# An RWKV-5 and sentence-level MoE kernel: opening re-ordered, logits read in PSUM, w1 loaded in two halves

## Chip, cores and metric

The kernel runs on one core of one Trainium2 chip. The metric is the device time of that core in microseconds (us), the median over several executions. Two parts of an execution are told apart throughout. The **opening** goes from the start to the first expert matmul job (called the first job below). The **packed part** goes from there to the end of the span. All moments are counted from the start of the span of the profiled execution; the span is some 1.7 us shorter than the device time. **Whole clock** and **half clock** are stretches in which the profile shows a granted TensorE clock of 1.0 and of 0.5. The **index** is the number of the chosen expert (`idx`), which the loads of w1 and w2 wait for.

## The reference

Four sequences of 768 steps with 8 heads of 48 run through a linear attention with decay; then each whole sequence goes to one of 8 experts. Cut to what matters:

```python
for t in range(S):                                   # S = 768
    cur = einsum('bhd,bhe->bhde', u[None] * k[t], v[t])
    y[:, :, t] = einsum('bhd,bhde->bhe', r[t], state + cur)
    state = w[None, :, :, None] * state + einsum('bhd,bhe->bhde', k[t], v[t])
x = y as (B, S, 384)
logits = x.mean(axis=1) @ w_gate                     # one expert for a whole sequence
e = argmax(logits); gate_w = softmax(logits)[e]
out = gate_w * (relu(x @ w1[e]) @ w2[e])             # w1 384x1024, w2 1024x384
```

## The kernel before

A sequence is cut into three groups of 256 steps, so there are twelve groups, 0 to 11, and four gates. For one group TensorE transposes the scaled k and r (`twp`), ScalarE copies the result to SBUF (`kr`), VectorE forms `prod` for the bonus, TensorE makes scores (`at`), VectorE masks them (`gt`), TensorE adds up y and the state `s`, VectorE forms the state `st`, ScalarE copies y (`xn`), and TensorE turns it back (`xp`, copied to `xt`). After the third group of a sequence the gate picks an expert. Its work is then cut into jobs of matmuls (`hp` for w1, `op` for w2), which fill TensorE while the next sequence's groups run.

The first sequence has no expert work to run beside it. There the author writes the order by hand and puts `fill` matmuls (zeros times zeros) into the gaps, meant to keep TensorE's clock up (in e5 below, with 19 more of them, half clock shrank from 20.5 us in e2 to 3.4).

```python
pp_tw  = tile_pool(bufs=1, space=PSUM)      # one bank: transposes, also xp
pp_at  = tile_pool(bufs=1, space=PSUM)
pp_moe = tile_pool(bufs=2, space=PSUM)      # two banks: hp, op, logits, fills, some twp
...
load(0); load(1)                            # each loads k, r, v of a group
wg = ...                                    # gate weights
for g in range(2, AHEAD): load(g)
fill(4, 512); ...; fill(7, 512)
...
def transposes(g, c):
    if c and g < NB + 2:                    # NB = 3: groups 0..4, second half, in pp_moe
        fill_bank()
        twp = pp_moe.tile(...)
    else:
        twp = pp_tw.tile(...)
    ...                                     # eight 128x128 transposes
    nc.scalar.copy(kts[g][:, :, :, c, :], tw)
    nc.vector.tensor_mul(prods[g][:, :, c], tw[:, 0:NP], rts[g][:, :, :, c, :])
...
def gate(b):
    lgp = pp_moe.tile([128, 512], FP32, tag="moe", name=f"lgp{b}")
    ...                                     # three small matmuls
    lg = gpool.tile([128, E], FP32, tag="lg", name=f"lg{b}")
    nc.vector.tensor_copy(lg, lgp[:, 0:E])
    nc.vector.max(out=top8, in_=lg)
    nc.vector.max_index(out=idx8, in_max=top8, in_values=lg)
def gate_weight(b):                         # in the packed part: after scores and bonus
    nc.vector.tensor_scalar_mul(negmax, top8[:, 0:1], -1.0 / S)
    nc.scalar.activation(out=exps, in_=lg, func=ACT.Exp, bias=negmax, scale=1.0 / S)
    ...
def mm1(b, w1, ht, ft, sb):                 # w1 is one tile [128, 3, 1024]
    nc.tensor.matmul(out=hp[:, 0:SB], lhsT=w1[:, ct, ft::NFT], rhs=...)   # NFT = 8
...                                         # the opening, cut to groups 0 to 3
prep(0); transposes(0, 0); transposes(0, 1); fill(4, 512); prep(1); scores(0, 0)
prep_v(0); ...; fill(5, 512); scores(0, 1); bonus(0, False); ...
transposes(1, 0); transposes(1, 1); scores_v(0, 1, True); ...
fill(3, 512); scores(1, 0); scores_v(0, 0, True); transposes(2, 0); fill(1, 512)
scores(1, 1); bonus(1); ...; transposes(2, 1); prep_v(2); fill(2, 512)
add_bonus(0); evac_y(0, 0); inter(0, 1); evac_y(0, 1)
scores(2, 0); scores_v(1, 1, True); backs(0); ...
prep_r(3); prep_v(3); ...                   # v of group 3 converted ahead of the gate
outputs(2, ...); pool_sum(0); transposes(3, 0); gate(0); weights(0); ...; gate_weight(0)
transposes(3, 1); fill(2, 256); scores(3, 0); fill(2, 256); scores(3, 1); bonus(3)
```

Of the kernel before, what the change touches and what calls it, by code (L numbers as in the profile page):

```python
# [18 lines left out]
def kernel(  # L19
# [52 lines left out]
    def load(g):  # L72
        b, gi = divmod(g, NB)
        for name, src in (("k32", k), ("r32", r), ("v32", v)):
            t = inp.tile([128, H, 2, D], FP32, tag=name, name=f"{name}_{g}")
            nc.sync.dma_start(
                out=t.rearrange("q h c d -> q h (c d)"),
                in_=src[b, :, L * gi : L * gi + L, :].rearrange("h (q c) d -> q h (c d)", c=2),
            )
            raw[name, g] = t  # L80
# [17 lines left out]
    load(0)  # L98
    load(1)
    wg = const.tile([128, NCT, E], FP32, tag="wg", name="wg")  # L100
    nc.sync.dma_start(out=wg, in_=moe_w_gate.rearrange("(p ct) e -> p ct e", p=128))
    for g in range(2, AHEAD):
        load(g)
# [16 lines left out]
    fill(7, 512)  # L120
# [75 lines left out]
    s_ps, xts, carry, tcols = {}, {}, {}, {}  # L196
# [31 lines left out]
    def transposes(g, c):  # L228
        if c and g < NB + 2:
            fill_bank()  # L230
            twp = pp_moe.tile([128, 2 * NP, 128], BF16, tag="moe", name=f"twp{g}_{c}")
        else:
            twp = pp_tw.tile([128, 2 * NP, 128], BF16, tag="tw", name=f"twp{g}_{c}")
        for o, src in ((0, kp[g % NR]), (NP, rp[g % NR])):
            for p in range(NP):
                nc.tensor.transpose(  # L236
                    out=twp[:, o + p, :],
                    in_=src[:, c, 2 * p : 2 * p + 2, :].rearrange("s a b -> s (a b)"),
                    identity=ident,
                )  # L240
        if c == 0:
            kts[g] = work.tile([128, 2 * NP, 2, 2, 64], BF16, tag="kr", name=f"kr{g}")
            rts[g] = kts[g][:, NP : 2 * NP]
            prods[g] = work.tile([128, NP, 2, 2, 64], BF16, tag="prod", name=f"prod{g}")
        tw = twp.rearrange("q o (j i) -> q o j i", j=2)
        nc.scalar.copy(kts[g][:, :, :, c, :], tw)  # L246
        nc.vector.tensor_mul(prods[g][:, :, c], tw[:, 0:NP], rts[g][:, :, :, c, :])  # L247
# [60 lines left out]

    def inter(g, j):
        st, rt = sts.pop((g, j)), rts[g]  # L310
        yj = ys[g][j]
        for p in range(NP):
            nc.tensor.matmul(  # L313
                out=yj[:, 96 * p : 96 * p + 96],
                lhsT=rt[:, p, j].rearrange("q c i -> q (c i)"), rhs=st[:, p, :],
                start=(j == 0 and p == 0), stop=False, skip_group_check=True,
            )
# [10 lines left out]
    def scores_v(g, j, first):  # L328

        gi = g % NB  # L330
        if j:
            ys[g] = [
                pp_y.tile([128, 512], FP32, tag=f"y{i}", name=f"y{i}_{g}") for i in range(2)]
        gt, vb, yj = gts[g], vbs[g], ys[g][j]
        o = 1 - j
        with_state = not (o == 1 and gi == NB - 1)
        if o == 0:
            b = g // NB
# [8 lines left out]
        sp = s_ps[g // NB]  # L347
        q, qo = slice(64 * j, 64 * j + 64), slice(64 * o, 64 * o + 64)

        def y_mm(i):  # L350
            h, c = divmod(i, 2)
            p, a = divmod(h, 2)
            nc.tensor.matmul(  # L353
                out=yj[:, D * h : D * h + D],
                lhsT=gt[q, p // 2, a, p % 2, c, :], rhs=vb[q, c, h, :],
                start=(first and i == 0), stop=(c == 1), skip_group_check=True,
            )

        def s_mm(i):
            p, c = divmod(i, 2)  # L360
# [4 lines left out]
                start=(gi == 0 and o == 0 and i == 0), stop=(c == 1), skip_group_check=True,  # L365
            )

        for i in range(H):
            y_mm(2 * i)
            if with_state:  # L370
                s_mm(i)
            y_mm(2 * i + 1)
        if not with_state:
            return
        st = work.tile([128, NP, 2 * D], BF16, tag="st", name=f"st{g}_{o}")
        nc.vector.tensor_mul(  # L376
            st, sp[:, 0 : 2 * D * NP].rearrange("q (p e) -> q p e", p=NP),
            wcmask if o else bmask.rearrange("q p a d -> q p (a d)"),
        )
        if o:  # L380
            carry[g // NB] = st
# [4 lines left out]
    def evac_y(g, j):  # L386
        if j == 0:
            xns[g] = work.tile([128, 2, DM], BF16, tag="xn", name=f"xn{g}")
        nc.scalar.copy(xns[g][:, j, :], ys[g][j][:, 0:DM])  # L389

    def backs(g):
# [3 lines left out]
        xn, sp = xns.pop(g), s_ps[b]  # L395
# [7 lines left out]
        for j in range(2):  # L403
            for ct in range(NCT):
                o = DM + 2 * NB * ct + 2 * gi + j
                nc.tensor.matmul(
                    out=sp[:, o : o + 1], lhsT=xn[:, j, ct::NCT], rhs=ones_col,
                    start=False, stop=True, skip_group_check=True,
                )
        nc.scalar.copy(xts[b][:, :, L * gi : L * gi + L], xp)  # L410
        for d in (vbs, kts, rts, prods, gts, vts, ys):
            d.pop(g, None)

# [13 lines left out]
    def gate(b):  # L427
# [7 lines left out]
        lg = gpool.tile([128, E], FP32, tag="lg", name=f"lg{b}")  # L435
        nc.vector.tensor_copy(lg, lgp[:, 0:E])  # L436
# [19 lines left out]
    jobs = []  # L456

    def weights(b):
        idx8 = gates[b][0]
        ev = nc.gpsimd.value_load(idx8[0:1, 0:1], min_val=0, max_val=E - 1)  # L460
        w1 = wpool.tile([128, NCT, F], BF16, tag="w1", name=f"w1_{b}")
        nc.gpsimd.dma_start(  # L462
            out=w1.rearrange("p ct f -> p (ct f)"),
            in_=moe_w1[ds(ev, 1)].rearrange("o (p ct) f -> p (o ct f)", ct=NCT))
        w2 = wpool.tile([128, NFT, DM], BF16, tag="w2", name=f"w2_{b}")
        nc.gpsimd.dma_start(
            out=w2.rearrange("p ft m -> p (ft m)"),
            in_=moe_w2[ds(ev, 1)].rearrange("o (p ft) m -> p (o ft m)", ft=NFT))
# [11 lines left out]
    def mm1(b, w1, ht, ft, sb):  # L480
        hp = pp_moe.tile([128, 512], FP32, tag="moe", name=f"hp{b}_{ft}_{sb}")
        for ct in range(NCT):
            nc.tensor.matmul(  # L483
                out=hp[:, 0:SB], lhsT=w1[:, ct, ft::NFT],
# [56 lines left out]
    def outputs(g, gaps=None):  # L541

        gaps = gaps or [lambda: None] * 3
        if g % NB:
            inter(g, 0)
        scores_v(g, 0, g % NB == 0)
        add_bonus(g)
        evac_y(g, 0)
        gaps[0]()
        inter(g, 1)  # L550
        evac_y(g, 1)
        gaps[1]()
        backs(g)
        gaps[2]()

    def gap():
        fill(1, 256)


    prep(0)  # L560
    transposes(0, 0)
    transposes(0, 1)
    fill(4, 512)
    prep(1)
    scores(0, 0)
    prep_v(0)
    load(4)
    late_constants()
    fill(5, 512)
    scores(0, 1)  # L570
    bonus(0, False)
    prep(2)
    vt_mul(0)
    transposes(1, 0)
    transposes(1, 1)
    scores_v(0, 1, True)
    prep_v(1)
    load(5)
    fill(3, 512)
    scores(1, 0)  # L580
    scores_v(0, 0, True)
    transposes(2, 0)
    fill(1, 512)
    scores(1, 1)
    bonus(1)
    prep_k(3)
    transposes(2, 1)
    prep_v(2)
    fill(2, 512)
    add_bonus(0)  # L590
    evac_y(0, 0)
    inter(0, 1)
    evac_y(0, 1)
    scores(2, 0)
    scores_v(1, 1, True)
    backs(0)
    gap()
    inter(1, 0)
    scores_v(1, 0, False)
    scores(2, 1)  # L600
# [4 lines left out]
    bonus(2, None)  # L605
    prep_r(3)
    prep_v(3)
    prep_k(4)
    backs(1)
    gap()  # L610
    scores_v(2, 1, True)
    outputs(2, [gap] * 3)
    pool_sum(0)
    transposes(3, 0)
    gate(0)
    weights(0)
    prep_r(4)
    prep_v(4)
# [4 lines left out]
    for g in (6, 7, 8):  # L623
        load(g)
    transposes(3, 1)
    fill(2, 256)
    scores(3, 0)
    fill(2, 256)
    scores(3, 1)
    bonus(3)  # L630

    for g in range(NB, N):
# [8 lines left out]
        if n1:  # L641
            transposes(g + 1, 0)
        slot()
        scores_v(g, 1, True)
        slot()
        if n1:
            transposes(g + 1, 1)
        if gi:
            inter(g, 0)
        scores_v(g, 0, gi == 0)  # L650
# [55 lines left out]
```

## Time and profile before

| kernel before | value | where it is read |
|---|---|---|
| device time, median (lowest to highest) | 154.73 us (154.41 to 156.17) | three runs |
| span of the profiled execution | 152.64 us | page |
| first job | 45.04 us | timeline of TensorE |
| packed part | 107.60 us | difference |
| half clock | 34.5 to 41.3 us | stretches by engine |

The prediction shows the slices, the stretches behind them and the chain. Three more lines serve the comparison. From the page's groups of the kernel before (line, engine, operation, names, shapes, count; busy us and mean ns of one; idle time before them): the weight loads of the w1 jobs take 148 ns each.

```profile
L483 PE MATMUL hp<-xt,w 128*128 128x384 bf16 x192 | 41.4, 334 | 1.3 <-DVE lg L436 0.3
L483 PEld LDWEIGHTS <-w 128*128 128x128 bf16 x192 | 25.0, 148 | 8.1 <-issue 4.4
```

From the timeline of the kernel before at the first gate (start, duration, engine, line, operation, names, shapes, count, and in brackets the idle time ahead of it with what ended it): the index is ready at 33.72 us, the second `kr` of group 3 follows at once, and the first masking of group 3 starts 2.03 us after the index.

```profile
34.02 0.99 ACT L246 COPY kr<-twp 128x1024 bf16<-128x1024 bf16 x1
...
35.75 1.23 DVE L268 TENSOR_TENSOR gt<-at,mask 128x1024 bf16<-128x1024 f32 x1 [0.28 <-PE at L260]
```

### The profile page before, as it was taken

To read this page: it belongs to the slowest core of one execution; us is meant where nothing else is said; L and a number is where in the kernel's file an instruction comes from. 1 tells how busy PE (TensorE), PEld (TensorE's weight loads), DVE (VectorE), ACT (ScalarE), POOL (GpSimd) and SP (SyncE) were. 2 spreads that over 40 slices of the span, in tenths; PEclk is the share of its full clock that TensorE was granted. 3 is DMA by queue.
4 is the path that set the end of the run, shared out by engine and by line. 5 is a ranking of instruction groups with operands and counts; after the bars stand their busy time and mean duration, and the time that the engine had idled before them with its cause. 6 is when DMAs were issued, how large, how long until landed. Compare 5 with 4: busy or idle time off the path is not lost.

```text
span 152.6 us, 4539 instructions
## 1 busy us (share of the span) xinstructions
PE 139.5 (91%) x1951; PEld 97.9 (64%) x1951; DVE 74.4 (49%) x164; ACT 83.6 (55%) x144; POOL 68.5 (45%) x62
## 2 busy tenths in 40 slices
PE   6999877956989999999999999999999999999991
PEld 2266645644767878766677877666777765676560
DVE  7837796125465654754548456465562321121110
ACT  0976567351356766546476784563664543556231
POOL 4169659207976839289292862963021020000000
PEclk9999999995599999999999999999999999999999
DMA  2999998303999999999991000998020079960034
GB/s 59 301 322 321 279 268 226 99 0 92 227 215 297 249 312 269 293 214 210 215 376 48 4 0 4 153 195 267 22 93 4 0 111 208 161 247 0 0 126 185
DMA packets 41464, 25.47 MB, mean 167 GB/s; under 512 B 38755, under 2 KB 39012, under 8 KB 41444
## 3 DMA queue, kind: packets, MB, share of 16 engines
q1 hardware_dynamic: 39460, 18.89, 42.9%
q0 software_dynamic: 1152, 6.29, 22.3%
q8 instruction: 15, 0.25, 0.6%
q10 hardware_dynamic: 832, 0.00, 0.3%
q14 instruction: 5, 0.04, 0.1%
HBM read 26.76 MB, written 4.72 MB: 206 GB/s over the span
## 4 chain that ended last, share of the span: by engine, by line
PE 78%; DVE 10%; ACT 8%; issue 2%; DVEq 0%
PE op L503 21%; PE hp L483 21%; PE twp L236 7%; PE at L260 5%; DVE gt L268 5%; PE fill L113 5%; PE y L353 5%; ACT kr L246 4%; PE s L361 2%; PE xp L402 2%; ACT ht L490 2%; PE y L313 2%; PE y L323 2%; DVE ht L492 1%; DVE st L376 1%
## 5 line engine op out<-in xcount | busy, mean ns | idle before, releaser
L483 PE MATMUL hp<-xt,w 128*128 128x384 bf16 x192 | 41.4, 334 | 1.3 <-DVE lg L436 0.3
L503 PE MATMUL op<-w,ht 128*128 128x384 bf16 x192 | 34.9, 326 | 0.1
L246 ACT COPY kr<-twp 128x1024 bf16<-128x1024 bf16 x24 | 24.1, 1011 | 18.4 <-PE twp L236 18.4
L268 DVE TENSOR_TENSOR gt<-at,mask 128x1024 bf16<-128x1024 f32 x24 | 29.3, 1221 | 8.8 <-PE at L260 8.6
L490 ACT ACTIVATE ht<-hp 128x384 bf16<-128x384 f32 x48 | 23.4, 491 | 17.8 <-PE hp L483 17.1
L483 PEld LDWEIGHTS <-w 128*128 128x128 bf16 x192 | 25.0, 148 | 8.1 <-issue 4.4
L305 POOL TENSOR_TENSOR vt<-vb,tcol 128x768 bf16<-128x768 bf16 x11 | 16.3, 1477 | 25.4 <-DVE tcol L297 25.4
L503 PEld LDWEIGHTS <-ht 128*128 128x128 bf16 x192 | 17.3, 97 | 11.1 <-issue 0.8
L247 DVE TENSOR_TENSOR prod<-twp,kr 128x512 bf16<-128x512 bf16 x24 | 10.2, 424 | 27.8 <-ACT kr L246 27.8
L199 POOL TENSOR_TENSOR kp<-k,dk 128x768 bf16<-128x768 f32 x11 | 20.0, 1816 | 1.4 <-DMA k<-in_k_dram 1.4
L199 POOL TENSOR_TENSOR rp<-r,dr 128x768 bf16<-128x768 f32 x11 | 20.0, 1820 | 0.0
L510 ACT ACTIVATE ob<-op,gw 128x384 f32<-128x384 f32 x16 | 9.3, 581 | 13.2 <-PE op L503 12.9
L113 PE MATMUL fill<-zero 128*128 128x512 bf16 (+1 forms) x45 | 14.5, 430 | 1.9 <-DVE zero L85 1.3
L353 PEld LDWEIGHTS <-gt 64*128 64x128 bf16 x384 | 11.5, 94 | 5.0 <-issue 3.9
L492 DVE TENSOR_SCALAR ht<-hp 128x384 bf16<-128x384 f32 x16 | 8.9, 554 | 11.7 <-PE hp L483 11.5
L353 PE MATMUL y<-vb,gt 64*128 64x48 bf16 x384 | 14.1, 182 | 0.4 <-ACT xn L389 0.4
L260 PE MATMUL at<-kr 48*64 48x128 bf16 x384 | 10.5, 229 | 3.6 <-ACT kr L246 1.7
L389 ACT CAST xn<-y 128x384 bf16<-128x384 f32 x24 | 11.1, 480 | 4.1 <-PE y L323 3.5
L462 POOL DMA_DIRECT2D w<-in_moe_w_dram x4 | 2.5, 623 | 22.5 <-DVE gw L452 7.8
L260 PEld LDWEIGHTS <-kr 48*64 48x64 bf16 x384 | 7.0, 110 | 8.2 <-issue 6.2
L410 ACT COPY xt<-xp 128x768 bf16<-128x768 bf16 x12 | 9.6, 798 | 4.3 <-PE xp L402 4.3
L361 PE MATMUL s<-vb,kp 64*128 64x96 bf16 x160 | 10.5, 208 | 0.4 <-DVE st L376 0.4
(73 smaller groups left out, 155.6 us busy)
## 6 DMA issues: line engine op xcount, KB each, us to landing
w<-in_moe_w_dram POOLq DMA_DIRECT2D x8, 768.0 KB, 10.2
k<-in_k_dram SPq DMA_DIRECT2D x12, 384.0 KB, 5.1
r<-in_r_dram SPq DMA_DIRECT2D x12, 384.0 KB, 5.8
v<-in_v_dram SPq DMA_DIRECT2D x12, 384.0 KB, 5.7
out_dram<-ob SPq DMA_DIRECT2D x11, 384.0 KB, 5.6
out_dram<-ob SPq DMA_DIRECT2D x2, 192.0 KB, 1.9
wuT<-in_w_dram ACTq DMA_DIRECT2D x2, 0.8 KB, 3.6
wuT<-in_u_dram ACTq DMA_DIRECT2D x2, 0.8 KB, 4.1
```

The costliest lines, as they stand in the source:

```text
L113: nc.tensor.matmul(out=fills[-1][:, 0:cols], lhsT=zero[:, 0:128], rhs=zero[:, 0:cols], start=True, stop=True)
L199: eng.tensor_mul(dst[:, cs, :, 0:D].rearrange("q c h d -> q h c d"), src[:, :, cs, :], dec[:, :, cs, :])
L246: nc.scalar.copy(kts[g][:, :, :, c, :], tw)
L260: nc.tensor.matmul(out=at[64 * j : 64 * j + 64, a, pp, cs, :], lhsT=kt[q, p, j, cs, :], rhs=rt[q, p, j].rearrange("q c i -> q (c i)"), sta ...
L268: nc.vector.tensor_mul(gts[g][:, rnd].rearrange("q a p c t -> q (a p) c t"), at.rearrange("q a p c t -> q (a p) c t"), mask.rearrange("q n ...
L305: nc.gpsimd.tensor_mul(vt, vbs[g].rearrange("q c h d -> q (c h) d"), tcol.to_broadcast([128, 2 * H, D]))
L353: nc.tensor.matmul(out=yj[:, D * h : D * h + D], lhsT=gt[q, p // 2, a, p % 2, c, :], rhs=vb[q, c, h, :], start=(first and i == 0), stop=(c ...
L361: nc.tensor.matmul(out=sp[:, 96 * p : 96 * p + 96], lhsT=kp[g % NR][qo, c, 2 * p : 2 * p + 2, :].rearrange("s a b -> s (a b)"), rhs=vb[qo, ...
L389: nc.scalar.copy(xns[g][:, j, :], ys[g][j][:, 0:DM])
L483: nc.tensor.matmul(out=hp[:, 0:SB], lhsT=w1[:, ct, ft::NFT], rhs=xts[b][:, ct, SB * sb : SB * sb + SB], start=(ct == 0), stop=(ct == NCT - 1),
L490: nc.scalar.activation(out=o, in_=hp[:, 0:SB], func=ACT.Relu)
L503: nc.tensor.matmul(out=op[:, 0:DM], lhsT=ht[:, ft, 128 * si : 128 * si + 128], rhs=w2[:, ft, :], start=(ft == 0), stop=(ft == NFT - 1),)
```

## The change

Its intent is to shorten the opening: k and r of the first groups are loaded ahead of v, VectorE takes over some evacuations, the stages of groups 1 and 2 are taken apart and interleaved anew, the logits are read where they lie in PSUM rather than copied, and w1 comes in two halves, so that the first jobs can start on the first half. The diff, cut to its core (helpers split without a change of their operations are left out, and so is w2, whose rows are loaded in an order that fits the halves):

```diff
-    load(0)
-    load(1)
+    load(0, "kr")
+    load(1, "kr")
+    load(0, "v")
+    load(2, "kr")
+    load(1, "v")
+    load(2, "v")
     wg = ...
-    for g in range(2, AHEAD):
-        load(g)
+    load(3)
...
-    fill(7, 512)
+    fill(5, 512)
...
-    def transposes(g, c):
-        if c and g < NB + 2:
+    def transposes(g, c, eng=None):
+        if c and g < NB:
             fill_bank()
             twp = pp_moe.tile(...)
...
-        nc.scalar.copy(kts[g][:, :, :, c, :], tw)
-        nc.vector.tensor_mul(prods[g][:, :, c], tw[:, 0:NP], rts[g][:, :, :, c, :])
+        if eng is nc.vector:
+            nc.vector.tensor_copy(kts[g][:, :, :, c, :], tw)
+        else:
+            nc.scalar.copy(kts[g][:, :, :, c, :], tw)
+        tws[g, c] = tw
+
+    def prod(g, c):
+        nc.vector.tensor_mul(prods[g][:, :, c], tws.pop((g, c))[:, 0:NP], rts[g][:, :, :, c, :])
...
-        lg = gpool.tile([128, E], FP32, tag="lg", name=f"lg{b}")
-        nc.vector.tensor_copy(lg, lgp[:, 0:E])
+        lg = lgp[:, 0:E]
...
-        w1 = wpool.tile([128, NCT, F], BF16, tag="w1", name=f"w1_{b}")
-        nc.gpsimd.dma_start(out=w1..., in_=moe_w1[ds(ev, 1)]...)
+        w1 = []
+        for fh in range(2):
+            t = wpool.tile([128, NCT, HF], BF16, tag=f"w1_{fh}", name=f"w1_{b}_{fh}")
+            nc.gpsimd.dma_start(out=t, in_=moe_w1[ds(ev, 1)]...[:, :, HF * fh : HF * fh + HF])
+            w1.append(t)
...
-                out=hp[:, 0:SB], lhsT=w1[:, ct, ft::NFT],
+                out=hp[:, 0:SB], lhsT=w1[ft // 4][:, ct, ft % 4 :: 4],
```

The new opening from group 1 to group 3 (cut; the old order is above):

```python
prod(1, 0); scores(1, 0); scores_v(0, 0); add_bonus(0); prep_v(1)
evac_y(0, 0); inter(0, 1); evac_y(0, 1)
prod(1, 1); bonus(1); transposes(2, 0); transposes(2, 1); load(4); load(5)
scores(1, 1); pool_mms(0); prod(2, 0); turn_back(0); prep_k(3)
inter(1, 0); scores_v(1, 1); prod(2, 1); scores(2, 0); bonus(2, False)
...
evac_y(1, 1); together([], state_mms(2, 0)); ...; scores(2, 1); ...
inter(2, 1); fill(1, 512); ...; evac_y(2, 1, nc.vector); fill(1, 256)
pool_mms(2); pool_sum(0); turn_back(2); gate(0); weights(0); gate_weight(0)
...
prep_v(3); transposes(3, 0); prod(3, 0); fill(2, 512); transposes(3, 1); prod(3, 1)
...; fill(4, 512); scores(3, 0); fill(3, 512); bonus(3); scores(3, 1); fill(2, 512)
```

## The prediction

> **What bounds the kernel now.** I read the page's slices first, then the stretches by engine, then the chain that ended last, then the timeline around the gates. From about 45 us on TensorE is the bound; before that no engine is, and a chain of short steps across engines sets the pace. Rows of the page (busy tenths and granted clock in 40 slices of 3.8 us):
>
> ```profile
> PE   6999877956989999999999999999999999999991
> PEclk9999999995599999999999999999999999999999
> ```
>
> Slices 8 and 9 of TensorE are 5 and 6, and just behind them stand two slices of half clock. The stretches by engine (columns: us, then busy of PE, PEld, DVE, ACT, POOL, then clock, DMA share, GB/s):
>
> ```profile
> 31.00:34.50 3.50, 2.07 (x24) 1.77 (x24) 1.28 (x8) 1.71 (x4) 0.00 (x0) 0.99 0.00 0
> 34.50:37.90 3.40, 2.05 (x43) 1.35 (x43) 1.84 (x4) 0.51 (x1) 2.56 (x3) 0.50 0.35 79
> 37.90:41.30 3.40, 3.36 (x47) 2.49 (x44) 2.01 (x4) 1.01 (x1) 3.40 (x4) 0.50 1.13 242
> 48.10:120.00 71.90, 71.40 (x1160) 53.67 (x1153) 39.26 (x79) 44.79 (x78) 38.92 (x30) 1.00 0.64 162
> ```
>
> TensorE is 60% busy for one stretch, the clock then halves for two, and from 48 us TensorE is 99% busy. So the time is (start of the first expert job, 45.0 us) + (107.6 us of packed work to the end at 152.6), and the change can act on either term. The chain in order of time between the first gate and that job:
>
> ```profile
> 31.06 0.62 PE twp L236 x8
> 31.71 1.02 ACT kr L246
> 32.75 0.42 DVE prod L247
> ...
> 33.81 0.30 ACT exps L448
> 34.11 0.91 ACT kr L246
> 35.02 0.04 issue
> 35.06 0.67 PE at L260 x12
> ...
> 44.69 0.42 PE at L260 x16
> 45.11 0.64 PE hp L483 x3
> ```
>
> Every link is a transpose, its evacuation, a score or its masking; none is the wait for w1, which landed at 43.5 us (issue 35.3). The chances of gain lie in starting `hp` earlier, the dangers in anything put into the packed 107.6 us. The timeline after the second gate shows such a place:
>
> ```profile
> 63.63 1.48 PE L503 MATMUL op<-w,ht 128*128 128x384 bf16 x8
> ...
> 65.14 0.62 DVE L513 TENSOR_SCALAR ob<-op,gw 128x384 f32<-128x384 f32 x1
> 65.14 0.81 PE L503 MATMUL op<-w,ht 128*128 128x384 bf16 x4
> ...
> 65.93 0.30 ACT L448 ACTIVATE exps<-lg,negmax 128x8 f32<-128x8 f32 x1 [2.64 <-DVE negmax L446]
> ```
>
> The second `op` starts at 65.14 while VectorE evacuates the first, so they lie in two banks; the gate's exponential comes 0.8 us later.
>
> [...] half clock from 34.5 to 41.3 us, 6.8 us or two windows, after a window 60% busy; the one from 24.2 to 27.6 us, 72% busy, cost nothing. [...] `prod` of 512 takes 0.42 us, `gt` of 1024 fp32 1.22[...]. [...] This bears on w1, whose columns are read at a step of 8 elements before and 4 after. The trace shows slower loads (144 ns against 97 for `op`) but not slower matmuls: single starts within a group are 162 ns apart for both. The loads are hidden.
>
> **The change part by part.**
>
> Loads. Loads land 1.2 us apart (r0 6.5, v0 7.8, r1 10.2, v1 11.4). Taking v0 and v1 back brings k1 from about 9.1 to 7.8 us and r1 to 9.0; GpSimd's scalings (1.82 us each, four in a row from 9.16) start at 7.85 and end at 15.1 rather than 16.3. v0 lands near 10.2, when ScalarE is ready for it. Gain at the second group: up to 1.2 us.
>
> First group. Two fills fewer let the transposes go at 6.95 instead of 7.67. The first evacuation on ScalarE ends at 9.1, the second on VectorE at 9.65 instead of 10.7 behind the first. So the first score ends at 10.3 (11.35 before), its masking at 11.6 (12.6). The two `prod` (0.84 us) now stand before the second masking, so that ends at 13.65 (14.4), and the bonus and the transposes of group 1 wait for them. The gain has shrunk to 0.7 us at `kr` of group 1 (ends 15.15, before 15.8), 1.0 at its first masking (starts 15.65, before 16.65).
>
> Groups 1 and 2. From there VectorE's new order decides: masking 15.65-16.87, `st` 17.4, `prod` 17.85, then bonus, sixteen transposes of group 2 (0.9 us), and only then the second score of group 1, so its masking runs 19.5-20.7 (before 19.3-20.5). The back-transpose of group 0 waits in its bank for `prod` of group 2 (21.1), `st` of group 1 ends at 22.95 (before 22.93). The early gain is spent. Adding `prod` 0.42, masking 1.22, `tcol`, two `st` (0.55), masking to 27.6, the y products and the two evacuations of group 2, now side by side, the sums end near 30.3 us (before 30.5).
>
> Gate. Its matmuls no longer stand behind group 3's transposes: 30.6-31.4 instead of 31.5-32.3. VectorE is free, needs no copy (0.17), and has the index at 31.95 instead of 33.7: 1.8 us earlier, and w1 is requested at 33.5 instead of 35.3. This buys nothing directly, since `hp` did not wait for w1.
>
> Group 3. ScalarE now has `exps` (32.15-32.45), the cast of v3 (0.84, before in the opening) and then `kr`: first to 34.3. The second transpose lies in the same bank as the first, so it follows `prod` (34.8), and `kr` ends at 36.35: 1.3 us later than before (35.0). From there at full clock: score 0.5, masking 1.22, score 0.45, fills 0.43, transposes 0.5, `kr` 1.05, `prod` 0.47, transposes 0.5, `kr` 1.05, `prod` and `st` 1.0, masking 1.25, score 0.45: 8.85, `hp` at 45.2 (before 10.0 us, half of it at half clock). But TensorE idles from 32.5 to 34.8, so a window only about 50% busy or less is there again and the clock should halve once; the eleven large fills then make the next window busy, so for one window, not two. That costs 0 to 0.9 us. `hp` at 45.2 to 46.1: opening +0.2 to +1.1, say +0.6.
>
> Gates 2 to 4. The logits now stay in PSUM until `exps`, which comes after the bonus. In the built program the gate's bank is 7 and both following tiles are in 6 (second gate: `op` 0 and 1; third: `hp` 7_0 and 7_1); at the fourth the gate has 6 and three `hp` in a row have 7. One bank where two alternated: the second gate waits out one evacuation (0.62 + 0.04 us), the third 0.5, the fourth two (about 1.2) less the 0.26 us that `hp` waited there for the copy, 0.9. Sum 2.1 us, all on TensorE in the packed part.
>
> w1 in halves. More and shorter rows for GpSimd to issue; the two issues took 0.59 and 0.53 us before, three take perhaps 1.2 us more (estimate from these), which may push `vt` behind its use (it was ready 0 to 0.4 us ahead at 69.3 and 98.3): 0 to 0.4 us. The first half landing earlier meets no wait.
>
> Sum: 154.7 + 0.6 + 2.1 + 0.1 = 157.5. Two allowances pull it down. Delays in the packed part give the other engines time to catch up (the chain has 10% VectorE and 8% ScalarE steps), worth perhaps 0.6. And I followed the opening by hand over some sixty steps, each uncertain by 0.05; its order and its fills are plainly tuned on the chip, so I shift by a further 1.2. I predict 155.7 us.
>
> **The rivals.** (a) The opening gains in full: the gate's 1.8 us and one window of half clock reach `hp`, which starts near 43, and the banks cost little. 152.5 to 153.5 us. For it: the halving of w1 makes sense only if `hp` became early enough to wait for it. Against: `kr` of group 3 behind `exps`, v3 and a shared bank. (b) The bank of the logits becomes the new wait, and the opening gains nothing: 157 to 158. For it: bank numbers, and the place of `exps` behind the bonus. Against: some of it hides behind other waits. (c) The clock falls twice or longer[...]: another 1 us, and a wider spread than 154.4 to 156.2. (d) The smaller step in w1's columns speeds up 192 matmuls: if 45 ns each were exposed, 8 us; the equal 162 ns rule this out.
>
> **Range and chances.** Rival (a) at its best gives 152.5, (b) with (c) 158.5. 2% is 3.1 us: faster needs under 151.6, more than (a) offers; slower needs over 157.8, which (b) with a bad clock reaches. Range 153.0 to 158.2, faster 0.09, same 0.77, slower 0.14.
>
> **What would show each step.** First masking of group 0 starting near 10.3; index near 32; second `kr` of group 3 near 36.3; first `hp` between 44 and 46; after gates 2 and 3 a hole of 0.5 to 0.7 us in TensorE, ended by the evacuation; half clock for one window near 35; `hp` still 162 ns apart. I am wrong if `hp` starts before 43.5, if the clock stays whole throughout, or if TensorE shows no hole after the gates.

## The result and the profile after

The changed kernel took 160.72 us (160.29 to 161.26, four runs), the kernel before 154.63 us on the same chip (154.41 to 156.17, four runs). The ratio is 1.037 (95% interval 1.030 to 1.045): slower by over 2%. Ratios here are the mean time of one kernel's fast runs over that of the other's fast runs of the same rounds, so they are not quite the ratio of the medians. The results are correct.

Where the time went, from the timelines of the two profiled executions (us; a masking is named by its group and round):

| moment | before | after | difference |
|---|---|---|---|
| first masking, group 0 | 11.40 | 9.84 | -1.56 |
| first masking, group 1 | 16.65 | 14.99 | -1.66 |
| first masking, group 2 | 21.14 | 22.40 | +1.26 |
| index of the first gate | 33.72 | 34.20 | +0.48 |
| first masking, group 3 | 35.75 | 40.04 | +4.29 |
| first job | 45.04 | 48.84 | +3.80 |
| packed part | 107.60 | 110.77 | +3.17 |
| span | 152.64 | 159.61 | +6.97 |

So the opening gives the early gain back, and more, at two places (group 2, and between the index and group 3), and the packed part grew too. The first three rows are not all the change's doing: whole clock first came at 10.6 us in the execution before and at 7.8 us in that after (there the traces' records of the clock begin; in the execution before, fills of 512 columns start 0.43 us apart ahead of that moment and 0.21 us apart behind it, although the slices print a 9 from the start). In e4 (below), which is the kernel before up to the first gate, it came at 7.4 us, and the three maskings start at 10.62, 15.87 and 20.36 us; in e3, which is the kernel after up to the request of w1, it came at 10.6 us, with 10.27 and 15.41 us. So at a like start the gain is 0.8 to 1.1 us in group 0 and 0.9 to 1.2 in group 1, and group 2 is 2.0 us late. The slices of the page after (busy tenths of TensorE; clock granted, in tenths) show what the new feature is: four slices at 5 in a row where the kernel before has two, and one at 6 at about 129 us, where the kernel before has none.

```profile
PE   6978569988989999989999999999999699999991
PEclk9999965555799999999999999999999969999998
```

The stretches by engine (us; then busy time and count of PE, PEld, DVE, ACT, POOL; clock, DMA share, GB/s), first one of the kernel before, then those of the kernel after. They are cut every 3.41 us, counted from the moment at which the clock fell, 34.5 us before and 21.5 us after: from change to change, the clock's records in the two traces last 6.83, 23.89 and 112.64 us before, and 3.41, 13.65, 20.48, 27.31 and 85.33 us after, each a whole multiple of 3.41. A stretch of that length is called a **window** below.

```profile
24.20:27.60 3.40, 2.45 (x69) 1.61 (x62) 2.46 (x3) 2.29 (x4) 3.35 (x2) 1.00 0.80 210
```

```profile
18.09:21.50 3.41, 2.00 (x60) 1.54 (x57) 1.55 (x2) 2.39 (x4) 3.41 (x3) 1.00 1.04 272
...
24.92:28.33 3.41, 3.33 (x49) 2.56 (x45) 1.97 (x3) 1.08 (x3) 2.16 (x2) 0.50 0.57 151
28.33:31.74 3.41, 3.33 (x51) 1.97 (x50) 0.59 (x2) 1.10 (x2) 0.00 (x0) 0.50 0.02 5
31.74:35.16 3.42, 3.42 (x25) 2.94 (x25) 0.97 (x7) 1.67 (x3) 0.00 (x0) 0.50 0.00 0
...
38.57:41.98 3.41, 3.41 (x45) 1.55 (x43) 1.82 (x3) 0.19 (x1) 2.33 (x3) 0.50 1.16 208
```

The clock fell at 21.5 us, behind a window in which TensorE was 59% busy (2.00 of 3.41), and came back at 42.0 us only: 20.5 us, six windows. Three of the windows between are 98% to 100% busy without bringing it back. The window of the kernel before shown above was 72% busy (2.45 of 3.40), and the clock stayed whole.

What made TensorE quiet at 18.8 us is in its timeline after: the transposes of group 0 (`xp`) wait 1.42 us for `prod` of group 2, which still reads the one bank of `pp_tw`.

```profile
18.51 0.31 PE L439 MATMUL s<-ones_col,xn 128*128 128x1 bf16 x6
20.24 0.49 PE L455 MATMUL xp<-ident,xn 128*128 128x128 bf16 x6 [1.42 <-DVE prod L258]
```

The group-3 stage after, from the timeline: the cast of v (`vb`) stands ahead of the first `kr`, and the second transposes wait 1.27 us for `prod`, as both now use one bank. The masking starts 5.84 us after the index rather than 2.03.

```profile
34.45 0.82 ACT L228 CAST vb<-v 128x768 bf16<-128x768 f32 x1
...
35.18 1.01 ACT L254 COPY kr<-twp 128x1024 bf16<-128x1024 bf16 x1
...
36.70 0.59 PE L241 MATMUL twp<-ident,kp 128*128 128x128 bf16 x4 [1.27 <-DVE prod L258]
...
40.04 1.23 DVE L279 TENSOR_TENSOR gt<-at,mask 128x1024 bf16<-128x1024 f32 x1 [0.83 <-PE at L271]
```

In the packed part there are holes behind the gates, where the tile of the logits still holds one of the two banks. After the second gate, and after the fourth:

```profile
69.28 0.81 PE L558 MATMUL op<-w,ht 128*128 128x384 bf16 x4 [0.53 <-DVE ob L568]
```

```profile
125.71 0.65 PE L538 MATMUL hp<-xt,w 128*128 128x384 bf16 x3 [0.58 <-ACT ht L545]
127.01 2.78 PE L538 MATMUL hp<-xt,w 128*128 128x384 bf16 x9 [0.65 <-DVE negmax L495]
```

The second of these two shows what follows: nine matmuls take 2.78 us, since the clock was halved once more, from 127.3 to 130.7 us. The weight loads of the w1 jobs did get shorter, as the halves bring a step of 4 columns for one of 8: 117 ns for 148, while the mean of one `hp` looks no better here (336 ns for 334); at whole clock, in e7, it is 328.

```profile
L538 PE MATMUL hp<-xt,w 128*128 128x384 bf16 x192 | 41.5, 336 | 2.7 <-ACT ht L545 1.2
L538 PEld LDWEIGHTS <-w 128*128 128x128 bf16 x192 | 19.7, 117 | 13.7 <-issue 7.4
```

### The profile page after: what moved, and what is told of

Same layout as the page of the kernel before. It is cut to its first block, busy times and chain, and to the rows that moved or that the text cites. A ratio compares the mean times of both kernels' runs of the same rounds, so it can differ in the third digit from the quotient of the medians.

```text
span 159.6 us, 4534 instructions
## 1 busy us (share of the span) xinstructions
PE 143.9 (90%) x1944; PEld 94.9 (59%) x1944; DVE 74.9 (47%) x162; ACT 83.3 (52%) x142; POOL 73.4 (46%) x66
## 4 chain that ended last, share of the span: by engine, by line
PE 77%; DVE 11%; ACT 8%; issue 2%; ACTq 0%
PE op L558 21%; PE hp L538 20%; PE twp L241 7%; PE fill L118 5%; DVE gt L279 5%; PE at L271 5%; PE y L361 4%; ACT kr L254 3%; PE xp L455 3%; PE s L387 3%; ACT ht L545 2%; PE y L339 2%; PE y L349 2%; DVE prod L258 2%; PE lgp L481 2%
## 5 line engine op out<-in xcount | busy, mean ns | idle before, releaser
L558 PE MATMUL op<-w,ht 128*128 128x384 bf16 x192 | 35.5, 330 | 0.6 <-DVE ob L568 0.5
L254 ACT COPY kr<-twp 128x1024 bf16<-128x1024 bf16 x23 | 23.1, 1013 | 19.2 <-PE twp L241 19.1
L538 PEld LDWEIGHTS <-w 128*128 128x128 bf16 x192 | 19.7, 117 | 13.7 <-issue 7.4
L515 POOL DMA_DIRECT2D w<-in_moe_w_dram x8 | 6.4, 804 | 22.6 <-DVE gw L501 8.8
L118 PE MATMUL fill<-zero 128*128 128x512 bf16 (+1 forms) x38 | 14.0, 478 | 1.3 <-DVE zero L87 1.3
L432 ACT CAST xn<-y 128x384 bf16<-128x384 f32 x23 | 10.7, 479 | 6.3 <-PE y L349 3.8
L241 PE MATMUL twp<-ident,kp 128*128 128x128 bf16 x96 | 10.0, 230 | 1.8 <-DVE prod L258 1.8
(73 smaller groups left out, 157.5 us busy)
```

Source lines behind the costliest of these rows:

```text
L118: nc.tensor.matmul(out=fills[-1][:, 0:cols], lhsT=zero[:, 0:128], rhs=zero[:, 0:cols], start=True, stop=True)
L241: nc.tensor.transpose(out=twp[:, o + p, :], in_=src[:, c, 2 * p : 2 * p + 2, :].rearrange("s a b -> s (a b)"), identity=ident,)
L538: nc.tensor.matmul(out=hp[:, 0:SB], lhsT=w1[ft // 4][:, ct, ft % 4 :: 4], rhs=xts[b][:, ct, SB * sb : SB * sb + SB], start=(ct == 0), stop ...
L558: nc.tensor.matmul(out=op[:, 0:DM], lhsT=ht[:, ft, 128 * si : 128 * si + 128], rhs=w2[:, ft, :], start=(ft == 0), stop=(ft == NFT - 1),)
```

## The experiments

The theory after the first look had three parts. **Clock**: the hole at 18.8 us halves the clock, and the small matmuls that follow don't bring it back. **Group 3**: the cast and the shared bank delay the last stage ahead of the first job. **Hold**: the logits in PSUM cost holes behind the gates. The rivals were that w1 in halves is to blame, that the clock is a symptom and costs nothing on the path, and that the new order as such is worse. Fifteen kernels ran; all gave correct results.

In the profiled executions half clock lasted 3.4 us (e5), 6.8 (the kernel before), 13.6 (e1), 17.1 (e6), 20.5 (the kernel after and e2), 27.3 (e3) and 37.6 us (e12), again whole multiples of 3.41, to 0.1 us. Where the changes lie against the kernel's start differs: whole clock first came at moments between 7.4 and 10.7 us. One program gives a spread (the kernel before, in the seven runs beside e1 to e4: granted clock 0.934 to 0.974, 154.11 to 156.57 us), and the opening as a whole starts up to 0.4 us earlier or later (first masking of group 0 at 9.84 to 10.28 us in the runs of the new opening). An execution in which the clock fell is often classed slow; fast runs alone enter the ratios, and timelines are compared with that in mind.

**e1: fills in the first hole.** In the kernel after:

```diff
     scores(1, 1)
     pool_mms(0)
+    fill(5, 512)
     prod(2, 0)
```

> The changed kernel with five fills of 512 columns more, put where TensorE idled 1.4 us before the back-transpose of group 0 (18.8 to 20.2 us); nothing else. Theory 1 (the clock carries the loss of the opening: in the trace it is halved from 21.5 to 42.0 us, after a stretch with TensorE 59% busy): the clock is not halved at 21.5; it may fall later, so the half-clock time shrinks from 20.5 us to 7 to 14, the first expert job starts 1.5 to 3 us earlier than 48.8, and the time is 157.5 to 159.5. Rival (the order of VectorE and ScalarE steps makes the opening late, and the clock is only a companion): the first expert job stays within 0.5 us of 48.8 and the time at 160 to 161.

158.84 us (158.82 to 158.91), ratio 1.026 to the kernel before. The clock fell all the same, but later, from 26.5 to 40.1 us; the first job started at 47.84 rather than 48.84 us, 1.0 us earlier where 1.5 to 3 were expected. Filling that one gap did not keep the clock whole. The packed part took 109.3 us; there was no dip of the clock at 127 us in this execution, with the same held bank. So of the 110.8 us after, some 1.4 belong to that dip.

**e2: the copy of the logits back.** In the kernel after:

```diff
-        lg = lgp[:, 0:E]
+        lg = gpool.tile([128, E], FP32, tag="lg", name=f"lg{b}")
+        nc.vector.tensor_copy(lg, lgp[:, 0:E])
```

> The changed kernel with the copy of the logits out of PSUM put back, so that the gate's bank is free again after 0.17 us. Theory 1 (the held bank costs 0.4 to 0.6 us at the second and third gate and 1.4 us at the fourth, and the hole at the fourth halves the clock from 127.3 to 130.7 us): all three holes go, no half clock near 127, time 3.0 us shorter, 157.2 to 158.2. Rival (delays hide behind other waits, the clock there falls in any case): under 1 us shorter.

158.83 us (158.13 to 160.15), ratio 1.028. The packed part fell from 110.77 to 107.00 us: the holes are gone, and in the slices of e2 so is the dip at 127 us, while the half clock of the opening stays.

```profile
PEclk9999985555599999999999999999999999999998
```

Against e1, which has the holes and no dip, the hold costs 2.3 us (109.33 less 107.00).

**e3: w1 and w2 in single loads.** In the kernel after, `weights` and the column step of `mm1` as in the kernel before:

```diff
-                lhsT=w1[ft // 4][:, ct, ft % 4 :: 4],
+                lhsT=w1[:, ct, ft::NFT],
```

> The changed kernel with w1 and w2 loaded as in the kernel before, w1 in one piece. Theory 1: the halves neither help nor hurt, as no job waits for w1: 160.2 to 161.2. Rival (the longer issue on GpSimd, 2.4 us against 1.25, delays its scalings): 0.5 to 1 us shorter. Second rival (the early first half helps the first job): longer by 0.5 us or more.

163.42 us (162.31 to 164.51), ratio 1.053: slower still, so the halves are not the culprit. But the run does not say that they are worth 2.7 us. Up to the request of w1 the two programs are the same, and yet here the index was ready at 36.56 rather than 34.20 us. The clock had fallen at 17.4 instead of 21.5 us, and whole clock had first come at 10.6 instead of 7.8; from the index to the first job it took 14.78 us, in the kernel after 14.64. The packed part, which comes after all this, took 111.38 us for 110.77 in the kernel after, both with a dip of the clock behind the fourth gate. This confound is why the later runs compare at whole clock.

**e4: the hold alone, in the kernel before.**

```diff
-        lg = gpool.tile([128, E], FP32, tag="lg", name=f"lg{b}")
-        nc.vector.tensor_copy(lg, lgp[:, 0:E])
+        lg = lgp[:, 0:E]
```

> The kernel before with one thing of the change: the logits stay in PSUM until the exponential. Theory 1 (the held bank alone): 2 to 3.5 us longer than before, 156.7 to 158.2, holes in TensorE after gates 2 to 4. Rival (it costs only together with the new opening): within 0.7 us of before.

157.64 us (156.5 to 159.84), ratio 1.018 (1.006 to 1.030). The first job stays at 45.13 us and the packed part grows by 2.1, from 107.60 to 109.69 us. The hole of the prediction is there, as long as in the kernel after:

```profile
65.90 0.81 PE L502 MATMUL op<-w,ht 128*128 128x384 bf16 x4 [0.53 <-DVE ob L512]
```

So the hold is shown from both sides: taken out of one kernel (2.3 us) and put into the other (2.1 us).

**e5: the copy, and full-size fills at every quiet place of the opening.** Kernel of e2, with e1's fills and

```diff
     evac_y(1, 1)
+    fill(3, 512)
...
-    fill(1, 512)          # after inter(2, 1)
+    fill(3, 512)
...
-    fill(1, 256)          # after evac_y(2, 1)
+    fill(3, 512)
...
     gate(0)
+    fill(3, 512)
...
-    fill(2, 512)          # after prod(3, 0)
+    fill(6, 512)
```

> The changed kernel with the logits' copy back and nineteen more fills of 512 columns in the places where TensorE waits between 18 and 35 us, the order of all else unchanged. Theory (the clock): the half-clock time between 18 and 45 us falls from 20 us to under 7, the first expert job starts at 45.5 to 46.5 us (after: 48.8; with the copy alone 49.5) and the packed part after it stays 107.0, so 153.5 to 155.5 us. Rival (order of steps in groups 2 and 3): the clock is whole, but the first job still starts after 47.5, and the time is over 156.

157.37 us over all runs (155.34 to 159.5), ratio of the fast runs 1.015. Half clock remained for one window in the profiled execution (24.6 to 28.0 us), and the first job started at 46.65 us, 2.8 earlier than in e2 (49.46); 0.2 us of this lies in the start (first masking of group 0 at 9.84 and 10.05 us). The expected 153.5 to 155.5 us were met by one run of four, as half clock remained in all of them (granted clock 0.955 to 0.989). Work was added to TensorE, and the kernel got faster.

**e6: the copy, and the group-3 stage mended.** Kernel of e2, with

```diff
-        if c and g < NB:
+        if c and g < NB + 1:          # second transposes of group 3 get their own bank
...
     evac_y(1, 1)
+    prep_v(3)                         # cast of v ahead of the gate
...
-    prep_v(3)                         # after gate_weight(0)
```

> The changed kernel with the logits' copy back, and group 3's stage put back as it was before: the cast of v3 earlier and the second transpose in its own bank. No more fills. Theory: from the index to the first masking of group 3 the changed kernel takes 5.8 us and the kernel before 2.0; this gives back 2.0 to 3.0 us of it whatever the clock does, so the first job starts near 46.5 to 47.5 and the time is 155.5 to 157. Rival (that stage only waits for the clock): under 1 us against the run with the copy alone (158.8).

156.36 us (155.69 to 158.11), ratio 1.008 (0.997 to 1.019). First job at 47.23 us, 2.2 earlier than in e2. The index came at 34.60 us in both (34.61 in e2), so all of it lies behind the index: from there to the first job it took 12.63 us, in e2 14.85, most of that at half clock in both (22.4 to 42.9 us in e2, 22.5 to 39.6 here). The 2.2 us include that the clock came back one window sooner.

**e7: all three mended.** Kernel of e5 with e6's edit.

> The copy, the fills and group 3's stage together. Theory (the three terms add): the first job at 42.5 to 44 us, time 150.5 to 152.5, faster than both kernels. Rival (with the clock whole and group 3 early, some other wait, w1's landing or GpSimd's scalings of group 4, ends last): the first job not before 44.5, 153 or more.

153.35 us (153.23 to 155.74), ratio 0.989 (0.979 to 0.998): the first version ahead of the kernel before. Its slices show no half clock (granted clock 1.0 in the profiled execution):

```profile
PEclk9999999999999999999999999999999999999999
```

The first job starts at 44.66 us, 4.8 earlier than in e2. What the group-3 stage is worth at whole clock, e5 and e7 tell: from the index to the first job they took 13.11 and 12.14 us, so 1.0 us, against 2.2 at half clock. The other 3.8 of the 4.8 us are the clock's. The index came at 32.52 us, 1.2 earlier than in the kernel before, but the stretch from it to the first job is 0.8 longer (12.14 for 11.32). A part of that is merely moved, since the gate now stands ahead of the transposes of group 3. The time is over the expected 150.5 to 152.5 us: the figures of the expectation's rival came true, not those of the theory. The last wait isn't w1, whose first half landed at 41.3 us; but the second transposes of group 4, still in the shared bank, wait 0.57 us for `prod` at 40.55 us, and no run undoes that.

**e8: whole clock in the kernel before.** Larger fills where the kernel before has its small ones at group 3:

```diff
     transposes(3, 1)
-    fill(2, 256)
+    fill(6, 512)
     scores(3, 0)
-    fill(2, 256)
+    fill(5, 512)
...
     def gap():
-        fill(1, 256)
+        fill(2, 512)
```

> The kernel before with its fills between 27 and 37 us made larger, nothing else. Theory: its two windows of half clock go or shrink to one, the first job starts 0.8 to 1.3 us earlier than 45.0, time 153.0 to 154.0, and the spread of its runs narrows. Rival: the clock does not matter there, as ScalarE and VectorE set the pace: 154.3 to 155.

154.30 us (153.98 to 154.63), ratio 0.995 (0.988 to 1.003). Half clock all but vanished (granted clock 0.996 to 1.0), and the first job did not move: 45.10 us for 45.04. The rival has the outcome, but not the reason: from the index to the first job it took 10.59 us for 11.32, so whole clock gave 0.7 us there, while the index came 0.8 us later (34.52 for 33.72), behind the larger fills ahead of the gate. The fills that hold the clock stand on the path and take what they give; what remains is a narrower spread.

**e9: e7 with single loads of w1 and w2** (e3's edit in e7), the comparison that e3 could not be.

> The run with copy, fills and group 3's stage (153.35 us, clock whole in three of four runs), now with w1 and w2 each in one load as before. This asks again, at a whole clock, what the halves do, since the earlier run of that kind (163.4 us) had its clock halved 4 us earlier, in a part of the program that is the same in both. Theory 1 (the halves are worth nothing, no job waits for w1): 153.0 to 153.8 where the clock is whole. Rival (the halves help: w1 lands at 41.3 us in halves and some 43.5 in one piece, while the first job starts at 44.7): 0.5 us or more longer. Second rival (the issue of three loads on GpSimd costs): 0.5 us or more shorter.

154.97 us (153.8 to 156.23), ratio 1.003. Two of its four runs had whole clock, at 153.80 and 153.85 us, and three of e7's, at 153.23 to 153.37. The first job is in the same place (44.62 and 44.66 us) and the packed part longer by 0.5 us (107.52 and 107.02). That is no chance of one execution: without the hold, all nine profiled executions with halves have 107.00 to 107.06 us, e15 below included, and all four with single loads (the kernel before, e8, e9, e11) 107.52 to 107.60. The groups of e9 and then of e7, from 44 us on:

```profile
L535 PE MATMUL hp<-xt,w 128*128 128x384 bf16 x192 | 41.2, 333 | 1.3 <-DVE lg L486 0.3 <-ACT ob L562 0.2 <-DVE ht L544 0.2
```

```profile
L539 PE MATMUL hp<-xt,w 128*128 128x384 bf16 x192 | 40.4, 328 | 1.3 <-DVE lg L486 0.3 <-ACT ob L566 0.2
```

One `hp` takes 5 ns less with the halves, and the 192 together are busy for 0.8 us less, of which 0.5 reaches the end. The start of a job doesn't wait for w1 in either.

**e10: second score of group 1 ahead of VectorE's products.** In e7:

```diff
+    scores(1, 1)
     prod(1, 1)
-    bonus(1)
     transposes(2, 0)
     transposes(2, 1)
...
-    scores(1, 1)
+    bonus(1)
     pool_mms(0)
```

> The same kernel with the second score of group 1 ahead of its bonus and of group 2's transposes, as in the kernel before. Theory (the order in groups 1 and 2 gives back the early gain: the maskings of group 0 and the first of group 1 start 1.5 us earlier than before, but the first of group 2 at 22.6 against 21.1): masking of group 2 starts 1.5 to 2 us earlier, the first job near 43, time 151.5 to 152.2. Rival (GpSimd's vt and its four scalings, or the bonus, take the place as the last wait): within 0.5 us of 153.35.

154.25 us (153.43 to 155.41), ratio 0.998. The second masking of group 1 starts at 17.17 rather than 18.83 us, but the first of group 2 at 22.69, where it was (22.60), and at whole clock the time is no better than e7's (153.43 and 153.45 us). The order on VectorE is not what spends the early gain.

**e11: the first group's part of the change in the old order.** Kernel of e8 with the new load order, the second evacuation on VectorE, the masking of group 0 ahead of its products, the late constants moved up with these, and the fills 7 and 4 reduced to 5 and 2.

> The kernel before with the larger fills of the earlier run (154.3 us, clock whole), plus the change's new first group alone: the loads in the new order, the second evacuation on VectorE, masking ahead of the products, fewer early fills. Theory (the first group's gain is real and carried if the later order is the old one): maskings 1 us earlier through groups 0 to 2, first job near 44.2, time 153.0 to 153.7. Rival (the gain is lost in old order as well, as a later step on ScalarE or GpSimd sets the gate): 154.0 to 154.6.

153.44 us (153.31 to 155.68), ratio 0.994 (0.991 to 0.998). The profiled execution fell in the slow state, with half clock from 26.4 us on, so only its start is used: first maskings of groups 0, 1 and 2 at 10.04, 15.51 and 20.00 us, against 11.21, 16.47 and 20.96 in e8. In the old order about 1 us of the early gain is still there at group 2.

**e12: e7 with small fills.** All fills behind 18 us use a quarter of the array (64 x 64) for the same number of columns:

```diff
-            nc.tensor.matmul(out=fills[-1][:, 0:cols], lhsT=zero[:, 0:128], rhs=zero[:, 0:cols], ...)
+            nc.tensor.matmul(out=fills[-1][0:64, 0:cols], lhsT=zero[0:64, 0:64], rhs=zero[0:64, 0:cols], ...)
```

> The kernel with copy, fills and group 3's stage, whose fills after the first 18 us now use a quarter of the array (64 rows and 64 columns of it), of the same 512 columns of data[...]. Theory 1 (the throttle goes by the time that TensorE streams): the clock stays whole as with full fills, 153.2 to 153.6. Theory 2 (it goes by how much of the array works): the clock falls near 22 us and stays down for 10 us or more in most runs, mean granted clock under 0.97, time 155 to 158.

163.58 us (162.58 to 167.28), ratio 1.057 (1.053 to 1.061). The same instructions in the same order, with the same columns, cost 10 us more. In the profiled execution (slow state; but the clock was 0.887 to 0.926 in all six runs, against 0.978 to 1.0 in e7's four) the clock fell at 17.4 and was back at 55.0 us. The fall isn't the small fills' doing, since the first of them runs at 20.24 us, and in e3, with whole fills, it fell at 17.4 us too; there it was back at 44.7. Its slices and two stretches:

```profile
PEclk9999655555555899999999999999999999999999
```

```profile
34.50:37.90 3.40, 3.40 (x24) 1.24 (x22) 0.56 (x1) 0.48 (x1) 0.00 (x0) 0.50 0.00 0
37.90:41.30 3.40, 3.40 (x22) 2.43 (x21) 0.82 (x7) 1.10 (x2) 0.00 (x0) 0.50 0.00 0
```

TensorE is busy without a break in both, and the clock stays halved; from 27.6 to 48.1 us it is 98% to 100% busy at a granted clock of 0.50. In e7, with fills on the whole array, the same stretches are 79% to 99% busy at 1.00. So TensorE's busy time alone did not bring the clock back here. The part of the array that the fills use is all that the edit changed, and it counts in this kernel, at least in part.

Three more runs were made on what was still open: what spends the early gain, and the size of the halves.

**e13: first score of group 2 ahead of the back-transposes.** In e7:

```diff
     prod(2, 0)
+    scores(2, 0)
     turn_back(0)
...
     prod(2, 1)
-    scores(2, 0)
     bonus(2, False)
```

> The combined kernel of e7 with one move: the first score of group 2 goes ahead of the back-transpose of group 0 in TensorE's order. In e7 TensorE waits there for the product of group 2, then does back-transposes, state and y products, and only then this score, so its masking starts at 22.60 us although its transposed inputs were ready at 19.95 and VectorE stood idle from 20.4 to 21.8. If TensorE's order spends the early gain: that masking starts near 20.5, the index comes about 1 us earlier (31.5 rather than 32.5), the first expert job starts near 43.6 rather than 44.7, and the time is about 152.4. If the path to the gate runs through the state and the y products and not through this score: the masking starts near 20.5 all the same, but the index stays at 32.5, the first job at 44.7 and the time at 153.3.

152.69 us (152.58 to 155.68), ratio 0.986 (0.982 to 0.991), the fastest of all. The score and its masking in e7, then in e13, from the timelines:

```profile
21.70 0.42 PE L271 MATMUL at<-kr 48*64 48x128 bf16 x16
...
22.60 1.22 DVE L279 TENSOR_TENSOR gt<-at,mask 128x1024 bf16<-128x1024 f32 x1
```

```profile
20.00 0.42 PE L271 MATMUL at<-kr 48*64 48x128 bf16 x16
...
20.46 1.23 DVE L279 TENSOR_TENSOR gt<-at,mask 128x1024 bf16<-128x1024 f32 x1 [0.28 <-PE at L271]
```

The masking comes 2.14 us earlier, and the index and the first job 0.76 us earlier (31.76 for 32.52, 43.90 for 44.66). Of each, 0.2 us lies in the start (first masking of group 0 at 9.84 for 10.05), so the move itself is worth about 1.9 and 0.55 us. So the place of this score in TensorE's queue, behind a back-transpose that waits for a bank, spends part of the early gain. It is somewhat less than the full microsecond expected: beyond group 2 the state and y products have their own path.

**e14: e13 and e10 together.**

> e10 (second score of group 1 ahead of VectorE's products) with the same move of group 2's first score. If both orders together spend the early gain: masking of group 2 starts near 20.1, first expert job near 43.3, about 152.1 where the clock stays whole. If neither does: as e10, 153.4 at whole clock. In e10 half of the runs had one or two windows of half clock after 20.9 us[...]; this may come here too[...].

153.12 us (152.77 to 154.53), ratio 0.991. First masking of group 2 at 21.09, first job at 44.52 us: no better than e13 (of the 0.62 us by which the job is later, 0.44 are there at the first masking of group 0), so e10's order is worth nothing here either, and the expected 152.1 us was missed.

**e15: the halves alone, in e11.** e11 with w1 and w2 loaded as in the change.

> e11 (kernel before with the new load order, VectorE's second evacuation, the masking ahead of the products, and large fills at the group-3 stage) with w1 and w2 loaded as in the change. If the halves are worth the 0.5 us that e9 lost without them: the packed part from the first expert job to the end takes 107.0 us rather than 107.6, the mean of one hp matmul is 328 ns rather than 333, and the time is 152.9 where the clock stays whole (e11 153.4). If the halves are worth nothing by themselves, as the prediction said: 153.4 and 107.6.

154.90 us (153.83 to 155.15), ratio 0.998. The time is not what was expected: in this chip's six runs the clock was never whole for the entire execution (0.985 to 0.997; in the profiled one half from 40.5 to 43.9 us, just ahead of the first job at 46.19). The measure that doesn't depend on that, the packed part, is 107.06 us for 107.60 in e11, and one `hp` takes 328 ns: the 0.5 us of the halves is there in the old order too.

## Why the prediction was right or wrong

**First group: right.** The first masking was to start at 10.3 us, 1.05 earlier than before, and the first of group 1 1.0 earlier. They started at 9.84 and 14.99, and at a like start the gain is 0.8 to 1.2 us; the 1.6 and 1.7 of the table have luck in them. VectorE's evacuation, for which the prediction had the author's estimate, took 0.69 us, where ScalarE's of the same size beside it took 1.01. That the early gain would be spent was right as well, though group 2 came even later than before (by 2.0 us in the kernel after against e4, by 1.6 at whole clock in e7 against e8), and with a wrong reason in part: it was put down to VectorE's order, which e10 shows to be of no weight, while e13 finds it in TensorE's order and the held bank of the transposes. The wait of `xp` for `prod` of group 2 had been written down in the prediction, with its moment (21.1 us), as a matter of VectorE's sums only.

**Gate: the index at 31.95 us, wrong.** It was 34.20, as all of this, from 21.5 us on, ran at half clock; at whole clock (e7) it is 32.52.

**Group 3: right in kind.** The cast ahead of `kr`, the second transposes behind `prod`, `kr` at 36.35 us (in the profile it ended at 38.76, in the same order, at half clock). Undone, it gave 2.2 us at half clock (e6) and 1.0 at whole clock (e7 against e5), where 1.3 was predicted.

**The clock: the step that failed.** "[...] the clock should halve once; the eleven large fills then make the next window busy, so for one window, not two. That costs 0 to 0.9 us." It halved for six, from 21.5 us on. The prediction looked for quiet stretches near the gate only, where the kernel before had its own, and judged them by TensorE's share of busy time; that a busy window brings the clock back it had seen once, in that kernel (99% busy from 37.9 to 41.3 us, then whole clock). Two things were overlooked. The first is the hole at 18.8 us, which follows from the wait that the prediction itself had found. The second is that the clock stayed at 0.50 under the matmuls that follow, mostly small ones, though TensorE was 98% to 100% busy from 24.9 to 35.2 us; it came back at 42.0, behind seven fills of 512 columns between 37.5 and 41.4 us. With the first job at 48.84 us, where 45.2 to 46.1 was predicted, this is the largest miss: the opening cost 3.8 us and not 0.6. Mending the clock gave 2.8 us with one window left (e5 against e2), 3.8 with none (e7, less the 1.0 of group 3).

**Bank of the logits: right, with its size.** Predicted were holes of 0.66, 0.5 and 0.9 us, 2.1 in all. The holes in e4 are 0.53, 0.40 and 1.23 us (0.58 and 0.65); e4 measured 2.1 us in the packed part, e2 against e1 2.3. Not foreseen was the half clock behind the hole at the fourth gate, for one window (127.3 to 130.7 us in the kernel after): 1.4 us more, by the packed part of 110.77 us against e1's 109.33, which has the held bank but not that dip.

**w1 in halves: small, but of the other sign.** Predicted was a loss of 0 to 0.4 us and no gain from the smaller step, since single starts within a group are 162 ns apart for both steps. They are, in the median. The mean distance between consecutive `hp` starts, worked out from the traces of e9 and e7, is 192 and 186 ns: the median hid the minority of starts in which the load shows. Of 153 such distances, 20 lie between 215 and 230 ns in e9, and 20 between 185 and 200 in e7; that is close to the 33 ns by which a load got shorter (148 and 115). The trace of the kernel before had it (20 of 153 between 215 and 230 ns). Measured gain: 0.5 us.

**The allowances: unfounded.** 0.6 us for engines that catch up and 1.2 us for an opening "plainly tuned on the chip" pulled the sum from 157.5 to 155.7. Tuning is no argument for a rewritten order, least of all where whole clock first comes at anything from 7.4 to 10.7 us.

The sum for the profiled execution (span up by 6.97 us, predicted 1.0): 3.2 missed in the opening, 1.4 for the dip and 1.8 of allowances, less 0.6 for the halves (put down as a loss of 0.1, in truth a gain of 0.5), which makes 5.8 of the 6.0 missing. Rival (c), a clock that falls twice or longer, was named; it was given 1 us and should have had 3 to 4.

**What stays open.** What makes the clock fall and come back. TensorE's busy share of the window ahead does not tell. Half clock came behind windows that were 59% busy (18.1 to 21.5 us after), 61% (2.07 of 3.41; 31.0 to 34.5 us before) and 75% (24.4 to 27.8 us in e4), and did not come behind one at 72% (24.2 to 27.6 us before). For the way back it is no better: whole clock came behind a window 99% busy (37.9 to 41.3 us before) and one 100% busy (38.6 to 42.0 us after), but not behind three at 98% to 100% (24.9 to 35.2 us after), nor in e12 between 27.6 and 48.1 us, at 98% to 100%. That the share of the array that the fills use matters in this kernel is shown (e12 against e7); the rest is not.

## What to carry to other kernels

Before an order is changed that leaves TensorE a hole, ask what the hole does to the clock, and fill it with matmuls that use the whole array: 19 added fills made the first job 2.8 us earlier here (46.65 us in e5 for 49.46 in e2; though in the kernel before, e8, larger fills gained nothing), while with fills on a quarter of the array (e12) half clock lasted 37.6 us. Ask who reads a PSUM tile last: here a copy of 0.17 us that frees the bank was cheap against the holes of 0.40 to 1.23 us behind the late reader, 2.1 to 2.3 us for three gates. And compare runs at equal clock, or check that the identical part of two programs took the same time, before a difference is put down to an edit.
